# Seven-product second layer for one more token group, and weight sums read from whole chunks

## The chip, the cores and the metric

One NeuronCore of one Trainium2 chip runs the whole kernel. The metric is device time in microseconds (us) of one execution. Matrix work runs on TensorE (PE), elementwise work on VectorE (DVE), ScalarE (ACT) and GpSimd (POOL); SyncE (SP) issues every DMA, in program order, and where an issue has to wait for data or for a free buffer, everything behind it on that queue waits too.

## The reference

```
attn_out = softmax(q kT / 8 + mask) v        # 8 batches x 8 heads, 576 tokens, head size 64
x = attn_out as 4608 tokens x 512            # heads side by side
h = x @ w_in                                 # 512 -> 2048
g = max(h, 0) + alpha * min(h, 0)
out = g @ w_out                              # 2048 -> 512
```

Masks are a window of 32 keys for the first four heads, and every fourth key of the last 128 for the others. All is float32; the kernel gets float32 accuracy from a faster matrix format by splitting each operand into a high and a low part and running three matmuls (high*high, high*low, low*high) for one product.

## The kernel before

Tokens are cut in nine tiles of 512. Tiles 0 to 2 are computed in a first stage, with the conversion of the weights and most of the attention. Tiles 3 to 8 are computed two at a time in `paired_stage`: pairs of tiles at t = 3, 5 and 7, and for each pair two groups (`grp` 0 and 1) of 1024 hidden columns. So there are six rounds, (3,0), (3,1), (5,0), (5,1), (7,0), (7,1), each an h phase (first layer) and a y phase (second layer).

Every h phase multiplies blocks two by two with seven products in place of eight (a Strassen scheme): four units `i`, each with products `q` = 1, 7, 6, 2, 5, 3, 4, and each product six 128x512 matmuls. The products 3 and 4 of a unit run inside the next unit, and those of the last unit inside the y phase, so an h phase holds 26 products of its own. `phase_h` leaves g as it is; `seven_h` also makes the sums of g that a seven-product y phase needs.

The y phase comes in two forms. `phase_y` is the plain one: 4 blocks of output columns x 8 slices x 2 tiles x 3 passes = 192 matmuls, in 32 steps of six (a hook number `n` = 8c + j stands behind each step, and operations that are hung on it are issued there). `seven_y` uses the seven products: 28 steps of six = 168 matmuls, in the order `YSTEPS`. `SEVENS` says which rounds use it: before, the four at t = 5 and 7.

`seven_y` needs sums of blocks of w_out. `second_sum` makes one set of them (set i of 0 to 7; sets 4 to 7 serve `grp` 1, sets 0 to 3 `grp` 0): two loads into a buffer, a run of GpSimd operations, two stores to `wY` in DRAM. The four hook positions of a set are those of first load, second load with the GpSimd work, first store, second store. Both loads and stores are on SP's queue, so a store that waits for GpSimd holds up what is behind it.

The weights of both layers come to PE through a ring of ten 256 KB slots: `take` uses one, `feed` refills the slot just used with the unit ten further on.

The last twelve attention pairs (20 to 31) are spread over the paired stage. A pair has `scores` (PE), `maxima` (DVE, L286 and L289), `exponentials` (ACT, L299), `divisions` and `turns` (DVE, L306 to L314), `values` (PE, L276), `highs` (ACT, L383) and `lows` (DVE, L390), which copy the result out of PSUM. It has one k, one q and one v buffer: a pair loads the next pair's k and q (L201, L202) as soon as its own scores are done, and the next v (L209) after its own values. Before, round (3,0) holds five pairs, a pair every five steps of `phase_y`, values eight steps behind scores; (3,1) three; (5,0) three, one of them in the h phase; (5,1) one, in the h phase. Pairs in an h phase hold two PSUM banks for their values (`NARROW`), the others four.

Of the kernel before, what the change touches and what calls it, by code (L numbers as in the profile page):

```python
# [17 lines left out]
P = 128  # L18
# [7 lines left out]
HB = 9  # L26
# [11 lines left out]
NARROW = (28, 31)  # L38
# [29 lines left out]
def tile_window_attention_prelu_ffn(  # L68
# [34 lines left out]
    marks = dram.tile([2 * NC, 1], F32, name="marks")  # L103
    wY = dram.tile([NFP, 2, P, 2, 2, 2, P], F32, name="wY")
# [301 lines left out]
    class Conversion:  # L406
# [172 lines left out]
    SEVENS = {(NSTD + 2, 0), (NSTD + 2, 1), (NSTD + 4, 0), (NSTD + 4, 1)}  # L579
    for t in range(NSTD, NTILE, 2):  # L580
        for grp in range(NFP // GP):
            seq = []
            for i in range(GP):
                seq.append((i, 1))
                if i:
                    seq += [(i - 1, 3), (i - 1, 4)]
                seq += [(i, 7), (i, 6), (i, 2), (i, 5)]
            units += [wS[grp * GP + i, WBLOCK[q]].rearrange("p a n -> p (a n)") for i, q in seq]
            if (t, grp) in SEVENS:
                for i, q in YSTEPS:  # L590
                    if q == 0:
                        units += [wS[grp * GP + i, WBLOCK[q]].rearrange("p a n -> p (a n)") for q in (3, 4)]
                    elif q in YBLOCK:
                        h, odd = YBLOCK[q]
                        units.append(wY[grp * GP + i, h, :, :, odd].rearrange("p c a n -> p c (a n)"))
# [152 lines left out]
    class Seven(Four):  # L748
# [5 lines left out]
        def __init__(self, t, grp, i):  # L754
            super().__init__(t, grp, i)
            self.turn, self.grp = (grp + i) % 2, grp
# [19 lines left out]
        def s(self, n):  # L776
            k = 3 * self.i + self.ORDER.index(n)
            if k < 8:
                return small(k)
            if "x" not in extra:  # L780
                extra["x"] = const.tile([P, 4, TT], F32, tag="xB0", name=f"extra_{self.id}")
            return extra["x"][:, k - 8]
# [50 lines left out]
    def phase_h(t, grp, hooks):  # L833
# [3 lines left out]
        for i in range(GP):  # L837
            u = Four(t, grp, i)
            u.mm(1)
            u.snap(1)  # L840
            if last:
# [4 lines left out]
            if last:  # L846
                last.low(22)
                last.low(12)
            u.mm(6)
# [3 lines left out]
            for op in hooks.get((i, 6), ()):  # L853
                op()
            u.mm(2)
            u.add(11)
            if last:
                last.low(21)
            u.mm(5)
# [3 lines left out]
            for op in hooks.get((i, 5), ()):  # L863
                op()
# [58 lines left out]
    def phase_y(t, grp, u, hooks):  # L923

        end = grp + 1 == NFP // GP
        for c in range(NC):
# [23 lines left out]
            for tt in range(2):  # L950
                if not end:
# [11 lines left out]
    def seven_y(t, grp, us, hooks):  # L963
# [41 lines left out]

        def H(k, name):
# [5 lines left out]
        def T(k, name):  # L1012
# [17 lines left out]
            (3, 6): [lambda: put(21, "A"), H(3, "T4"), L(3, "T4")],  # L1030
            (3, 5): [lambda: put(22, "A")],
# [4 lines left out]
        for n, (i, q) in enumerate(YSTEPS):  # L1036
# [11 lines left out]
            else:  # L1048
# [3 lines left out]
                for c in range(2):  # L1052
                    for k, (a, e) in enumerate(PASSES):
                        b = 2 * c + a
# [8 lines left out]

    SUMS = {
# [3 lines left out]
    }  # L1068

    def second_sum(i, rooms):  # L1070
# [4 lines left out]
        def load(h):  # L1075
            if not room:
                room.extend(rooms())
            nc.sync.dma_start(
                out=room[h].rearrange("p c o a n -> p c (o a n)"),
                in_=wO[i // GP, 2 * h:2 * h + 2, i % GP].rearrange("c p o a n -> p c (o a n)"))  # L1080

        def last_load():
            load(1)

            def t(q):
                return room[q % 2][:, :, q // 2, 1]

            for x in room:
                nc.gpsimd.tensor_tensor(out=x[:, :, :, 1], in0=x[:, :, :, 0], in1=x[:, :, :, 1], op=ALU.add)  # L1089
            for out, x, y, op in ((3, 1, 3, ALU.add), (1, 0, 1, ALU.subtract), (0, 3, 0, ALU.subtract), (2, 2, 0, ALU.subtract)):  # L1090
                nc.gpsimd.tensor_tensor(out=t(out), in0=t(x), in1=t(y), op=op)  # L1091
            for x in room:
                nc.gpsimd.tensor_copy(out=x[:, :, :, 0].bitcast(F32R), in_=x[:, :, :, 1])
                nc.gpsimd.tensor_tensor(
                    out=x[:, :, :, 1].bitcast(F32R), in0=x[:, :, :, 1], in1=x[:, :, :, 0], op=ALU.subtract)

        def store(h):
            nc.sync.dma_start(
                out=wY[i, h].rearrange("p c o a n -> p (c o a n)"), in_=room[h].rearrange("p c o a n -> p (c o a n)"))
# [3 lines left out]
    def second_sums(hooks, at, spare):  # L1103

        for i, ats, k in SUMS.get(at, ()):
            ops = second_sum(i, (lambda: spare) if k is None else (
                lambda i=i, k=k: [gbuf([P, 2, 2, 2, P], F32, f"wy{i}_{a}", k + a) for a in range(2)]))
            for n, op in zip(ats, ops):
                hooks.setdefault(n, []).append(op)
# [26 lines left out]
    def attention_hooks(hooks, us, start, step):  # L1136
        def put(n, *ops):
            hooks.setdefault(min(n, GF * NC), []).extend(ops)

        lag = max(step + 2, 8)  # L1140
        for k, u in enumerate(us):
            n = start + step * k
            nxt = pairs.index(u) + 1

            def begin(u=u, nxt=nxt):
                u.scores()
                if nxt < len(pairs):
                    pairs[nxt].load_qk()
                u.maxima()
                u.exponentials()  # L1150

            def middle(u=u):
                u.divisions()
                u.turns()

            def end(u=u, nxt=nxt):
                u.values()
                if nxt < len(pairs):
                    pairs[nxt].load_v()
                u.highs()  # L1160
                u.lows()

            put(n, begin)
# [3 lines left out]
    def paired_stage():  # L1167
# [5 lines left out]
        both = const.tile([P, 2, 2, 2, 2, P], F32, tag="xB1", name="wy_spare")  # L1173
        spare = [both[:, h] for h in range(2)]
        early = second_sum(0, lambda: spare)
        late = []
        for t in range(NSTD, NTILE, 2):
            for grp in range(NFP // GP):
                ahead, hooks, seven = {}, {}, (t, grp) in SEVENS

                def put(hooks, u, ats, *tags):
                    for at, op in zip(ats, steps(u, *tags)):
                        hooks.setdefault(at, []).append(op)

                if t == NSTD:
                    us, todo = (todo[:5], todo[5:]) if grp == 0 else (todo[:3], todo[3:])
                    attention_hooks(hooks, us, *{5: (2, 5), 3: (3, 5)}[len(us)])
                    if grp == 0:
                        ahead[0, 5], ahead[1, 6], ahead[2, 5], ahead[3, 6] = ([op] for op in early)
                elif todo:  # L1190
                    free = YPAIRS[1 - grp]
                    put(ahead, todo.pop(0), ((0, 1), (0, 6), (0, 5), (1, 7), (2, 1)), free, free)
                    if grp == 0:
                        two, four = ("a1", "a3"), ("a1", "a3", "y0", "y1")
                        put(hooks, todo.pop(0), (9, 12, 13, 14, 18), two, four)
                        put(hooks, todo.pop(0), (16, 18, 19, 23, 26), ("y0", "y1"), four)
# [16 lines left out]
                second_sums(hooks, (t - NSTD, grp), spare)  # L1213
# [358 lines left out]
```

## Time and profile before

| What | Value |
|---|---|
| Median of three runs | 851.68 us (850.93 to 854.68) |
| The profiled execution: its own time | 848.32 us |
| The profiled execution: its span, first to last instruction | 846.5 us |
| PE busy | 832.0 us, 98% of the span |
| DVE, ACT, POOL busy | 71%, 52%, 16% |
| DMA moved | 182.43 MB, mean 216 GB/s |

The profile is of one execution; the table's first line is of other executions of the same program. Busy shares are means over stages of different kinds, so each stage has to be looked at by itself.

### The profile page before, as it was taken

The page shows a single profiled execution, that of the slowest core. Times are in us where ns is not written, and L with a number is a line of the kernel's source. Part 1 is how long each engine was busy: PE and PEld are TensorE (multiplying, and loading weights), DVE is VectorE, ACT ScalarE, POOL GpSimd, SP SyncE. Part 2 cuts the span into 40 slices and gives each one's busy share as a digit, 9 for nine tenths or more (in the row PEclk, how much of TensorE's full clock was granted, in tenths as well). Part 3 has the DMA queues.
Part 4 walks back from the last instruction along what each step waited for, and adds up shares of the span by engine and source line. Part 5 has one row for each costly group of instructions (what it writes and reads, how often), then busy time and mean ns, then how long its engine had stood idle before and what let it go on. Part 6 is the DMA issues. An engine that isn't in the chain of part 4 may idle for free.

```text
span 846.5 us, 20231 instructions
## 1 busy us (share of the span) xinstructions
PE 832.0 (98%) x8094; PEld 679.3 (80%) x8094; DVE 604.3 (71%) x1024; ACT 437.9 (52%) x1218; POOL 133.6 (16%) x132
## 2 busy tenths in 40 slices
PE   8889999999999999999999999999999999999998
PEld 5677888888888888888788878788888888888886
DVE  5987767676777668686627678698369978843982
ACT  7885766434343543565336642667266436634650
POOL 0000000200405250053900087000300000000000
PEclk9999999999999999999999999999999999999999
DMA  7753444125989965688886787867966686666664
GB/s 258 273 186 100 148 158 145 45 94 173 303 268 336 283 221 171 241 263 251 296 266 193 216 302 263 276 190 239 298 168 191 216 273 192 193 195 194 194 209 142
DMA packets 123515, 182.43 MB, mean 216 GB/s; under 512 B 9758, under 2 KB 69278, under 8 KB 123422
## 3 DMA queue, kind: packets, MB, share of 16 engines
q1 hardware_dynamic: 123422, 181.15, 67.0%
q8 instruction: 64, 1.05, 0.5%
q14 instruction: 29, 0.24, 0.1%
HBM read 139.17 MB, written 41.94 MB: 214 GB/s over the span
## 4 chain that ended last, share of the span: by engine, by line
PE 92%; DMA 3%; POOL 2%; DVE 1%; issue 1%; ACT 1%; SPq 0%; ACTq 0%; DVEq 0%
PE h L456 16%; PE y L504 15%; PE pA L670 15%; PE qA L1055 10%; PE y L935 9%; PE pC L670 8%; PE qC L1055 5%; PE pB L670 4%; PE o L329 3%; PE qB L1055 3%; PE s L227 2%; PE s L251 1%; PE o L276 1%; POOL wy L1091 1%; DMA w_dt.float<-qT 1%
## 5 line engine op out<-in xcount | busy, mean ns | idle before, releaser
L456 PE MATMUL h<-x,w_dt.float32r 128*128 128x512 f32 x576 | 141.3, 394 | 0.9 <-ACT x L383 0.8
L504 PE MATMUL y<-g,w_dt.float32r 128*128 128x512 f32 x576 | 138.3, 389 | 0.0
L456 PEld LDWEIGHTS h<-x,w_dt.float32r 128*128 128x128 f32 x576 | 107.2, 188 | 23.8 <-ACT x L383 0.9
L504 PEld LDWEIGHTS y<-g,w_dt.float32r 128*128 128x128 f32 x576 | 108.0, 188 | 22.4
L299 ACT ACTIVATE pr<-pr,nm 128x64 f32<-128x64 f32 x216 | 72.3, 338 | 57.4 <-DVE nm L289 57.4
L482 ACT CAST g<-m 128x512 fp32r<-128x512 f32 x48 | 29.7, 619 | 74.8 <-DVE m L477 71.8
L670 PE MATMUL pA<-parts_w,ring_w 128*128 128x512 f32 x228 | 56.7, 390 | 0.2 <-ACT stage L904 0.2
L670 PE MATMUL pA<-parts_w,ring_xA 128*128 128x512 f32 x228 | 56.4, 390 | 0.0
L670 PEld LDWEIGHTS pA<-parts_w,ring_w 128*128 128x128 f32 x228 | 42.6, 188 | 9.5 <-ACT stage L904 0.6
L670 PEld LDWEIGHTS pA<-parts_w,ring_xA 128*128 128x128 f32 x228 | 42.7, 188 | 8.9
L811 DVE TENSOR_TENSOR gp<-stage,gp 128x512 fp32r<-128x512 f32 x64 | 42.9, 684 | 2.8 <-ACT gp L807 2.8
L487 DVE TENSOR_TENSOR g<-m,g 128x512 fp32r<-128x512 f32 x48 | 33.6, 700 | 15.5 <-ACT g L482 15.4
L476 DVE TENSOR_SCALAR m<-h,al 128x512 f32<-128x512 f32 x27 | 20.2, 749 | 29.8 <-PE h L456 29.8
L807 ACT CAST gp<-stage 128x512 fp32r<-128x512 f32 x64 | 37.5, 618 | 7.6 <-DVE stage L804 6.4
L299 ACT ACTIVATION_READ_ACCUMULATOR pr<-pr,nm 128x1 f32 x216 | 40.9, 189 | 0.0
L935 PE MATMUL y<-gp,ring_w 128*128 128x512 f32 x168 | 40.7, 394 | 0.0
L1055 PE MATMUL qA<-gp,ring_w 128*128 128x512 f32 x162 | 39.1, 390 | 0.0
L554 POOL TENSOR_TENSOR wsum_xB<-w_dt.float32r 128x512 f32<-128x512 f32 x4 | 5.1, 1295 | 208.8 <-PE h L456 161.9
L935 PE MATMUL y<-gp,ring_xA 128*128 128x512 f32 x156 | 37.3, 393 | 0.0
L1089 POOL TENSOR_TENSOR wy<-wy 128x512 f32<-128x512 f32 x12 | 16.4, 1374 | 128.7 <-DMA wy<-wO 69.4
L935 PEld LDWEIGHTS y<-gp,ring_w 128*128 128x128 f32 x168 | 31.1, 188 | 6.5
L1055 PE MATMUL qA<-gp,ring_xA 128*128 128x512 f32 x150 | 36.2, 390 | 0.0
(177 smaller groups left out, 1687.2 us busy)
## 6 DMA issues: line engine op xcount, KB each, us to landing
ring_xA<-wS SPq DMA_DIRECT2D x67, 256.0 KB, 2.9
ring_w<-wS SPq DMA_DIRECT2D x66, 256.0 KB, 3.6
ring_g<-wS SPq DMA_DIRECT2D x35, 256.0 KB, 3.3
ring_w<-wO SPq DMA_DIRECT2D x34, 256.0 KB, 3.2
ring_xA<-wO SPq DMA_DIRECT2D x33, 256.0 KB, 3.0
wO<-w_dt.float32r SPq DMA_DIRECT2D x32, 256.0 KB, 4.6
wS<-wc SPq DMA_DIRECT2D x16, 512.0 KB, 4.6
k<-kT SPq DMA_DIRECT2D x24, 288.0 KB, 4.6
```

Source lines behind the costliest of these rows:

```text
L299: nc.scalar.activation(out=self.pr[:, r, :], in_=self.ps[r // CUT0][:, r % CUT0, :] if self.onto else self.pr[:, r, :], func=AF.Exp, bias= ...
L329: nc.tensor.matmul(self.po[u][e * D:(e + 1) * D, a:z, :], lhsT=self.v[rows, i, :], rhs=self.pt[rows, a * BK + (BQ if i else 0):z * BK - (B ...
L456: nc.tensor.matmul(ms[t, f], lhsT=weight(0, a, f)[:, c * P:(c + 1) * P], rhs=half(t, c)[:, e, :], start=(c == 0 and n == 0), stop=(c == NC ...
L476: nc.vector.tensor_scalar(out=m, in0=ps, scalar1=0.0, scalar2=al[:, f:f + 1], op0=ALU.min, op1=ALU.mult)
L482: nc.scalar.copy(out=g[:, 0, :], in_=ms[t, f])
L487: nc.vector.tensor_tensor(out=g[:, 1, :], in0=ms.pop((t, f)), in1=g[:, 0, :].bitcast(F32), op=ALU.subtract)
L504: nc.tensor.matmul(ys[t][c], lhsT=weight(1, a, f)[:, c * P:(c + 1) * P], rhs=g[:, e, :], start=(first and n == 0), stop=(last and n == 2),)
L670: nc.tensor.matmul(to, lhsT=w[:, (2 * a + c) * P:(2 * a + c + 1) * P], rhs=part_of(name, e)[:, c * TT:(c + 1) * TT], start=start and c == ...
L807: nc.scalar.copy(out=self.pair(n)[:, 0], in_=self.whole(n))
L811: nc.vector.tensor_tensor(out=p[:, 1], in0=self.whole(n), in1=p[:, 0].bitcast(F32), op=ALU.subtract)
L935: nc.tensor.matmul(ys2[tt], lhsT=w[:, k * P:(k + 1) * P], rhs=g[:, e], start=j == 0 and n == 0, stop=j == GF - 1 and n == 2)
L1055: nc.tensor.matmul(named(to)[c], lhsT=w[:, b * P:(b + 1) * P], rhs=rhs[:, e], start=begins and k == 0, stop=i == GP - 1 and k == 2, skip_g ...
```

## The change

1. Round (3,1) joins `SEVENS`: its h phase becomes `seven_h` and its y phase `seven_y`.
2. The seven-product sets are made for it in time: sets 4 and 5 in the h phase of (3,0), sets 6, 7, 0 and 1 in its y phase, sets 2 and 3 in the h phase of (5,0). Before, sets 0 to 3 were made in (3,0), 4 to 6 in (3,1), 7 in (5,0).
3. A set is no longer made from the stored high and low parts, which GpSimd had to add again (L1089). Each w_out chunk is stored whole, as `wW`, when it is converted; the loads of a set are half as big. `wY` is laid out so that a unit is one piece for each partition; `b` in `seven_y` follows.
4. (3,0) takes seven attention pairs in its y phase, one every four steps, values six steps behind scores; pair 27 goes to the h phase of (3,1) and becomes narrow; (5,0) and (5,1) keep theirs.
5. Temporaries: the third set of temporaries that does not fit (`further`) goes to other buffers; in (3,0), two blocks of partial sums go to DRAM (`part`) and are read back late in the y phase of (3,1) (`again`).

```diff
-NARROW = (28, 31)
+NARROW = (27, 28, 31)
...
+    wW = dram.tile([NFP, P, 2, 2, 2, P], F32, name="wW")
...
         def low(self):
             nc.vector.tensor_tensor(
                 out=self.dst[1], in0=self.a.bitcast(F32), in1=self.dst[0].bitcast(F32), op=ALU.subtract)
+            if self.which:
+                nc.sync.dma_start(
+                    out=wW[self.f // 2, :, :, self.f % 2].rearrange("p h c n -> p h (c n)"),
+                    in_=self.a.bitcast(F32).rearrange("p (h n) -> p h n", h=2))
...
-    SEVENS = {(NSTD + 2, 0), (NSTD + 2, 1), (NSTD + 4, 0), (NSTD + 4, 1)}
+    SEVENS = {(NSTD, 1), (NSTD + 2, 0), (NSTD + 2, 1), (NSTD + 4, 0), (NSTD + 4, 1)}
...
+        def further(self, k):
+
+            if self.t == NSTD and k in (1, 2):
+                if k == 2:
+                    return pr0.rearrange("q j k -> q (j k)")[:, :TT]
+                if "pt" not in extra:
+                    extra["pt"] = att.tile([P, HB * BK], F32, tag="pt", name=f"extra_{self.id}")
+                return extra["pt"][:, :TT]
+            if self.t == NSTD or self.grp == 0:
+                return partial(*((0, 1), (2, 0), (3, 0), (1, 1))[k])
...
+                if not end and tt and c < 2 and (t, 1) in SEVENS:
+                    o = ffp.tile([P, TT], F32, tag="m", name=f"ob_{t}_{c}_{tt}", bufs=5)
+                    nc.vector.tensor_copy(out=o, in_=ys2[tt])
+                    nc.sync.dma_start(out=part[c], in_=o)
+                    continue
...
             nc.sync.dma_start(
-                out=room[h].rearrange("p c o a n -> p c (o a n)"),
-                in_=wO[i // GP, 2 * h:2 * h + 2, i % GP].rearrange("c p o a n -> p c (o a n)"))
+                out=room[h][:, :, 1].rearrange("p o c n -> p o (c n)"), in_=wW[i, :, h].rearrange("p o c n -> p o (c n)"))
...
-            for x in room:
-                nc.gpsimd.tensor_tensor(out=x[:, :, :, 1], in0=x[:, :, :, 0], in1=x[:, :, :, 1], op=ALU.add)
...
-                if t == NSTD:
-                    us, todo = (todo[:5], todo[5:]) if grp == 0 else (todo[:3], todo[3:])
-                    attention_hooks(hooks, us, *{5: (2, 5), 3: (3, 5)}[len(us)])
-                    if grp == 0:
-                        ahead[0, 5], ahead[1, 6], ahead[2, 5], ahead[3, 6] = ([op] for op in early)
+                if (t, grp) == (NSTD, 0):
+                    us, todo = todo[:7], todo[7:]
+                    attention_hooks(hooks, us, 1, 4, 6)
+                    put(ahead, ((0, 6), (0, 5), (2, 1), (2, 7)), second_sum(4, at_place("xB1")))
+                    four = second_sum(5, at_place("xB1"))
+                    put(ahead, ((3, 1), (3, 6)), four[:2])
+                    put(hooks, (3, 4), four[2:])
+                    put(hooks, (6, 8, 11, 12), second_sum(6, at_buffers(6, 1)))
+                    put(hooks, (8, 10, 15, 16), second_sum(7, at_buffers(7, 3)))
+                    put(hooks, (12, 14, 19, 20), second_sum(0, at_place("xB1")))
+                    put(hooks, (16, 18, 23, 24), second_sum(1, at_buffers(1, 1)))
...
+                    put(ahead, ((1, 1), (1, 6), (2, 7), (2, 2)), second_sum(2, at_place("xB0")))
+                    four = second_sum(3, at_place("xB0"))
+                    put(ahead, ((3, 7), (3, 2)), four[:2])
+                    put(hooks, (2, 3), four[2:])
```

## Rows read from the trace of the kernel before

**Rows 1.** Page, part 1: busy time, share of the span and instructions of each engine.

```profile
PE 832.0 (98%) x8094; PEld 679.3 (80%) x8094; DVE 604.3 (71%) x1024; ACT 437.9 (52%) x1218; POOL 133.6 (16%) x132
```

**Rows 2.** Page, part 4: the chain that ended last, by engine.

```profile
PE 92%; DMA 3%; POOL 2%; DVE 1%; issue 1%; ACT 1%; SPq 0%; ACTq 0%; DVEq 0%
```

**Rows 3.** Chain in order of time: start, us, twelve matmuls in a row.

```profile
77.92 2.72 PE h L456 x12
```

**Rows 4.** Windows by phase: (3,0) whole, (3,1) h, y, (5,0) h, y, (5,1) h.

```profile
core 0: us, PE busy (x) PEld busy (x) DVE busy (x) ACT busy (x) POOL busy (x), PEclk, DMA share, GB/s
343.98:437.62 93.64, 93.64 (x1142) 75.92 (x1141) 59.79 (x108) 45.12 (x158) 41.13 (x40) 1.00 0.85 282
437.62:472.98 35.36, 35.36 (x158) 29.28 (x157) 23.24 (x35) 19.59 (x36) 0.00 (x0) 1.00 0.68 195
472.98:526.44 53.46, 53.46 (x674) 43.30 (x673) 40.28 (x64) 23.44 (x83) 34.40 (x29) 1.00 0.79 271
526.44:565.52 39.08, 38.74 (x313) 31.48 (x312) 31.06 (x51) 23.13 (x56) 1.59 (x2) 1.00 0.77 239
565.52:611.14 45.62, 45.62 (x494) 37.12 (x493) 30.17 (x57) 23.88 (x74) 9.51 (x10) 1.00 0.83 260
611.14:649.62 38.48, 38.41 (x313) 31.56 (x312) 28.46 (x50) 24.08 (x60) 0.00 (x0) 1.00 0.64 182
```

**Rows 5.** Timeline, (5,0) h: ACT and PE behind a store of sums.

```profile
533.00 0.59 ACT L904 COPY stage<-pA 128x512 f32<-128x512 f32 x1 [4.44 <-DMA wY<-wy]
...
533.64 3.02 PE L670 MATMUL pA<-parts_w,ring_w 128*128 128x512 f32 x12 [0.23 <-ACT stage L904]
```

**Rows 6.** Timeline, (3,0) y: a pair's values, copies out of PSUM, scores.

```profile
408.57 1.12 PE L276 MATMUL o<-pt,v 32*64 32x32 f32 x84
409.63 3.02 PE L935 MATMUL y<-gp,ring_xA 128*128 128x512 f32 x12
...
409.74 0.19 DVE L390 COPY raw_xA<-o 128x32 f32<-128x32 f32 x1 [3.56 <-PE o L276]
409.85 0.48 DVE L390 COPY raw_xB<-o 128x128 f32<-128x128 f32 x2
...
410.24 0.68 DVE L953 COPY py<-y 128x512 f32<-128x512 f32 x1
...
412.57 0.97 PE L251 MATMUL s<-k,q 64*32 64x64 f32 x72
```

**Rows 7.** Timeline of POOL: first and last operation after L1089, three sets.

```profile
365.05 4.18 POOL L1091 TENSOR_TENSOR wy_spare<-wy_spare 128x256 f32<-128x256 f32 x4
...
373.24 1.63 POOL L1094 TENSOR_TENSOR wy_spare<-wy_spare 128x512 fp32r<-128x512 f32 x1
...
407.56 0.73 POOL L1091 TENSOR_TENSOR wy<-wy 128x256 f32<-128x256 f32 x1
...
413.92 1.30 POOL L1094 TENSOR_TENSOR wy<-wy 128x512 fp32r<-128x512 f32 x1
...
516.53 1.69 POOL L1091 TENSOR_TENSOR wy<-wy 128x256 f32<-128x256 f32 x1
...
526.83 1.28 POOL L1094 TENSOR_TENSOR wy<-wy 128x512 fp32r<-128x512 f32 x1
```

**Rows 8.** Page, part 6: DMA issues, KB each, median us to landing.

```profile
ring_w<-wS SPq DMA_DIRECT2D x66, 256.0 KB, 3.6
...
wO<-w_dt.float32r SPq DMA_DIRECT2D x32, 256.0 KB, 4.6
```

**Rows 9.** Tile q, from 380 to 640 us.

```profile
DMA to landing us min/median/max: 4.2/4.7/5.7
```

**Rows 10.** Timeline of SP in (3,0) y: issues of k and q.

```profile
422.78 0.33 SPq L201 DMA_DIRECT2D k<-kT  x1
423.17 1.72 SPq L202 DMA_DIRECT2D q<-qT  x1
```

**Rows 11.** Timeline of DVE in (3,0) y: one operation, POOL idle, then busy.

```profile
393.53 0.76 DVE L308 TENSOR_TENSOR pr<-pr,rs 128x576 f32<-128x576 f32 x1
...
401.49 1.67 DVE L308 TENSOR_TENSOR pr<-pr,rs 128x576 f32<-128x576 f32 x1
```

**Rows 12.** Timeline of DVE: operations of the token parts, POOL idle and busy.

```profile
520.91 1.76 DVE L655 TENSOR_TENSOR parts_w<-raw_xA,parts_w 128x1024 fp32r<-128x1024 f32 x1
...
696.32 1.22 DVE L655 TENSOR_TENSOR parts_w<-raw_xB,parts_w 128x1024 fp32r<-128x1024 f32 x1 [1.48 <-ACT parts_w L652]
```

**Rows 13.** Windows of the first stage, where the weights are converted.

```profile
90.00:130.00 40.00, 40.00 (x178) 33.15 (x177) 29.45 (x47) 25.30 (x44) 0.00 (x0) 1.00 0.52 180
```

More of the change, by code (lines that the diff above doesn't have):

```diff
@@ L838, in phase_h, with more @@
             u = Four(t, grp, i)
+            def more(q):
+                for op in hooks.get((i, q), ()):
+                    op()
             u.mm(1)
             u.snap(1)
+            more(1)
             if last:
@@ L848, in phase_h @@
                 last.low(12)
+            more(7)
             u.mm(6)
@@ L852, in phase_h @@
                 last.high(21)
-            for op in hooks.get((i, 6), ()):
-                op()
+            more(6)
             u.mm(2)
@@ L858, in phase_h @@
                 last.low(21)
+            more(2)
             u.mm(5)
@@ L862, in phase_h @@
             u.add(22)
-            for op in hooks.get((i, 5), ()):
-                op()
+            more(5)
             last = u
@@ L1004, in whole_first, with again @@
                     nc.sync.dma_start(out=outT[c * P:(c + 1) * P, t * TT:(t + 1) * TT], in_=out(11, c))
+        def again():
+            if t == NSTD:
+                for c in range(2):
+                    nc.sync.dma_start(out=out(12, c), in_=part[c])
         def H(k, name):
@@ L1092, in last_load, with at_buffers, at_place, rooms @@
             for x in room:
-                nc.gpsimd.tensor_copy(out=x[:, :, :, 0].bitcast(F32R), in_=x[:, :, :, 1])
-                nc.gpsimd.tensor_tensor(
-                    out=x[:, :, :, 1].bitcast(F32R), in0=x[:, :, :, 1], in1=x[:, :, :, 0], op=ALU.subtract)
+                nc.gpsimd.tensor_copy(out=x[:, :, 0].bitcast(F32R), in_=x[:, :, 1])
+                nc.gpsimd.tensor_tensor(out=x[:, :, 1].bitcast(F32R), in0=x[:, :, 1], in1=x[:, :, 0], op=ALU.subtract)
         def store(h):
             nc.sync.dma_start(
-                out=wY[i, h].rearrange("p c o a n -> p (c o a n)"), in_=room[h].rearrange("p c o a n -> p (c o a n)"))
+                out=wY[i, h].rearrange("p o a c n -> p (o a c n)"), in_=room[h].rearrange("p o a c n -> p (o a c n)"))
         return lambda: load(0), last_load, lambda: store(0), lambda: store(1)
[L1103 to L1109, printed above, removed]
+    def at_buffers(i, k):
+        return lambda: [gbuf([P, 2, 2, 2, P], F32, f"wy{i}_{a}", k + a) for a in range(2)]
+    def at_place(tag):
+        def rooms():
+            if tag not in sets:
+                sets[tag] = const.tile([P, 2, 2, 2, 2, P], F32, tag=tag, name=f"wy_{tag}")
+            return [sets[tag][:, h] for h in range(2)]
+        return rooms
+    sets = {}
     def steps(u, *tags):
@@ L1134, in steps, with attention_hooks @@
         return begin, lambda: u.exponentials(0, CUT0), lambda: u.exponentials(CUT0), middle, end
-    def attention_hooks(hooks, us, start, step):
+    def attention_hooks(hooks, us, start, step, lag):
         def put(n, *ops):
-            hooks.setdefault(min(n, GF * NC), []).extend(ops)
-        lag = max(step + 2, 8)
+            hooks.setdefault(n, []).extend(ops)
         for k, u in enumerate(us):
+            begin, first, second, middle, end = steps(u, *((("a0", "a2"), ABANKS) if k == 0 else (ABANKS[2:], ABANKS) if k % 2 else (ABANKS[:2], ABANKS)))
             n = start + step * k
[L1143 to L1163, printed above, removed]
+            put(n, begin, first, second)
             put(n + step - 1, middle)
@@ L1190, in paired_stage @@
                 elif todo:
                     free = YPAIRS[1 - grp]
[L1192 to L1196, printed above, removed]
+                    put(ahead, ((0, 1), (0, 6), (0, 5), (1, 7), (2, 1)), steps(todo.pop(0), free, free))
```

26 lines of the change are left out of this document (13 added, 13 removed), and 3 rows, old and new, of the table SUMS.

## Prediction

> **What bounds the kernel now.** I read the page's busy shares first, then the chain that ended last, then windows cut at the phases, then the timelines of PE, POOL, DVE and SP in the rounds that change. PE is busy for 98% of the span [rows 1] and makes up 92% of the chain [rows 2]: the kernel ends when PE has worked off its queue. The engines beside it matter only where one makes PE wait. So the change is counted in PE time, and then each place where PE could be made to wait is looked at.
>
> PE's unit of work is a step of six 128x512 matmuls. Twelve in a row take 2.72 us [rows 3], so a step is 1.36 us and a matmul 0.227. The windows [rows 4] can be rebuilt from that. The h phase of (3,1) has 26 steps and no attention: 26 x 1.36 = 35.36, to the hundredth what its window shows. Round (3,0) has 26 + 2 + 32 = 60 steps, 81.60, and five pairs: (93.64 - 81.60) / 5 = 2.41 us of PE time for a pair. The y phase of (3,1) gives the same price: 53.46 - 34 x 1.36 = 7.22 for three pairs, 2.41 each. A pair inside an h phase costs more: (5,1) h is 38.48 - 35.36 = 3.12. And (5,0) h, the same work, takes 39.08, 0.60 more: there ACT sat 4.44 us until a store of sums had landed, and PE lost time behind it [rows 5]. In this accounting PE has no other slack in these rounds.
>
> **The change, part by part.**
>
> *The seven-product y of (3,1).* 192 matmuls become 168: 24 x 0.227 = **-5.44 us**. The h phase keeps its 26 steps.
>
> *Pair 27* moves from a y phase (2.41) to an h phase (3.12): **+0.71**. The two other pairs moved from (3,1) to (3,0) keep their price of 2.41, as both are y phases.
>
> *The sets leave the y phase of (3,1).* The store that ACT waited for at the start of (5,0) [rows 5] is then long done: **-0.60**, the difference of the two h phases above.
>
> *The seventh pair of (3,0)* has its values at hook 31, behind the last step. The next thing on PE is the first product of (3,1), which writes a bank that DVE copies these values out of. Before, one more step stood between. There [rows 6] PE goes on at 409.63 after a pair's values, and DVE's copies end at 409.85 + 0.48 = 410.33, 0.70 later; after its first copy alone (409.93) it would be 0.30. I take **+0.70**, as this pair's share in that bank is several pieces. These four give -4.63.
>
> *Seven pairs, one every four steps, in (3,0).* A pair comes every 4 x 1.36 + 2.41 = 7.85 us in place of 9.21. DVE and ACT have room: 59.79 and 45.12 us busy of 93.64 there [rows 4]. What gets tight is SP's queue. k and q of the next pair are issued once this pair's scores are done, and needed 7.85 - 1.1 = 6.7 us later (2.41 split as 0.97 to 1.12 [rows 6] gives 1.1 for scores, 1.3 for values). q takes 4.7 us to land, 5.7 at most [rows 9], and its own issue can take 1.72 [rows 10]. So little is left if anything stands in front of it, and the new stores do: hooks 12, 16 and 20 hold a set's second store, which waits for the end of that set on POOL, and the loads of k and q at hooks 13, 17 and 21 are behind them.
>
> Times from the start of the y phase: pair k (from 0) is scored at 5.44 + 7.85k - 1.3 for k of 1 or more, so pairs 4, 5 and 6 at 35.5, 43.4 and 51.2. Set 6's second load (hook 8) is queued behind the spill of the first block, which needs pair 0's values (end near 17.1), DVE's copies (0.7) and the block's copy (0.68) [rows 6]; issued near 18.9, landed near 22.3 (256 KB take 3.6 in the ring [rows 8], a little less at best). POOL then makes sets 6, 7, 0 and 1 back to back. Without L1089, which the change removes, a set takes p = 415.22 - 407.56 = 7.66 us in (3,0) y, 9.82 in (3,0) h and 11.58 late in (3,1) y, from start to end of its operations [rows 7]. Between POOL's end and q's issue come a store, a load or none, a feed and k, some 1.3 to 1.7 us at 0.33 to 0.4 each [rows 10], and q lands 4.7 later. So q of pair 4 is there at 28.7 + p, of pair 5 at 28.7 + 2p, of pair 6 at 28.3 + 3p, and PE's total loss is the largest of p - 6.8, 2p - 14.7 and 3p - 22.9. With p = 7.66 that is 0.9, and with landings of 5.7 it is 1.9; with p = 9.82 it is 6.6. From below it is nothing, if q is quicker by the 0.5 that its fastest landing (4.2) shows, and the load of set 6 too. POOL runs here beside the same DVE work as in the 7.66 row, only denser, so I take p near that row and a landing between the two: **+1.5**.
>
> DVE and POOL disturb each other: the multiplication L308 takes 0.76 alone and 1.67 beside POOL [rows 11]. The Trainium skill, "SBUF — State Buffer", section "Who interferes with whom", says why: a DVE operation with two SBUF inputs and a GpSimd operation that reads SBUF share one read interface, and the one that comes second waits for the whole of the other. By that rule each pair's L308 would add up to 0.76 to a set: p = 8.4, a loss of 2.3 in place of 0.9. The rows agree that DVE waits; they show 7.66 with such a pair beside it.
>
> *(5,0) h* now has pair 28, five operations of the token parts that came earlier before, and POOL's sets 2 and 3. DVE was busy 31.06 of 39.08 [rows 4]. Three of the five are DVE's, 1.22 each alone and 1.76 beside POOL [rows 12]: 3.7 to 5.3 us more, so 35 to 36 of 38.5. That fits in sum, but in unit 0 products 3 and 4 have to wait for ACT's copies, which stand behind exponentials and one such operation more. Between 0 (all covered) and 1.5 (one ACT and one DVE operation of the token parts late) I take **+0.4**. Set 3's last store must land before a unit of it is fed; by p = 11.58 that is just in time, so nothing.
>
> *The 16 stores of whole chunks* cost SP about 0.4 us each where the DMA share is 0.52 [rows 13], and land in 4.6 [rows 8]; the buffer they hold is reused over a step (5.44) later. I take 0; the other bound is 1 us, for the first three, which fall in the start. If DMA were full there, each would cost its own transfer. The new layout of `wY` and L1089's removal have no PE time of their own: POOL idles 84% of the span [rows 1].
>
> Sum: -5.44 + 0.71 - 0.60 + 0.70 + 1.5 + 0.4 = **-2.7 us**. The profiled execution took 848.32 (span 846.5), so 845.6. The median of the runs is 851.68; taken off that, **849.0 us**.
>
> **The rivals.**
>
> *All is hidden* (A): q always lands in time and (5,0) h runs free; -4.63 remains, to -5.3 if the values at hook 31 are covered too: 846.4 to 847.1. For it: PE waits for almost nothing today. Against: the 0.9 that the best row of p gives.
>
> *POOL's chain holds SP* (B), slower: place, the second store of sets 6, 7 and 0 in (3,0) y. If a set takes 9.82 as in the h phase, the loss is 6.6 and the time 851.68 - 4.63 + 6.6 + 0.4 = 854.1; at 11.58 it is 11.8, and 859.3. It makes the kernel slower than before from p = 9.1, and by over 0.5% from p = 10.5. Against: three sets in this very phase took about 7.66.
>
> *DVE binds (5,0) h* (C): if DVE's operations there all took their long form, about 1.5 to 4 us would be lost: 850 to 852.5.
>
> **How the numbers follow.** 0.5% is 4.3 us, about what a measurement of this kernel can tell from no change. My forecast 0.48 (losses of 0.5 to 4 in all, 847.5 to 851), A 0.32, C 0.10, B 0.10. A is faster by over 0.5%; the forecast and C are within it; B is slower, nearly all of it by over 0.5%. So faster 0.32, same 0.58, slower 0.10. The range goes from A's lower end, 846.4, to 853.0, which holds C and leaves out B.
>
> **What would show it.** (3,1) y without attention should be 28 + 2 steps, 40.8 us, and (3,1) h 38.5 plus the loss at its first product. (3,0) should be 81.60 + 7 x 2.41 = 98.5, and what is above it is loss: in PE's waits at the scores, with DMA as the releaser, and in SP's waits for POOL at the stores. POOL's sets should take 7 to 8.5 us there. (5,0) h should be 38.5 plus at most 1.5. I would be wrong most of all if SP does not get held (then A), or if p is above 9 (then B).

## The result, and the profile after

The changed kernel takes **862.88 us** (median of 4 runs, 861.6 to 863.85) against 852.03 for the kernel before in the same job: 1.0143 of it, 95% interval 1.0117 to 1.0169. It is slower by 10.9 us. The forecast was 849.0 with a range up to 853.0. The profiled execution took 863.11 (span 861.3), against 848.32.

The page's busy shares, against [rows 1]:

```profile
PE 834.3 (97%) x8070; PEld 677.9 (79%) x8070; DVE 624.5 (73%) x1052; ACT 444.2 (52%) x1232; POOL 108.2 (13%) x116
```

The page's chain by engine, against [rows 2]:

```profile
PE 84%; DVE 8%; ACT 3%; DMA 3%; issue 2%; SPq 0%; ACTq 0%; DVEq 0%
```

PE has 24 matmuls fewer, and is busy longer, which points to a lower clock in places. DVE had 1% of the chain and has 8% now. Windows of the kernel after, cut at the phases as in [rows 4]: (3,0) y, (3,1) h, (3,1) y, (5,0) h, (5,0) y; (3,0) h, from 349.08, takes 35.36 as planned:

```profile
384.44:458.77 74.33, 67.01 (x1297) 52.44 (x1296) 43.43 (x95) 31.86 (x166) 35.72 (x40) 0.95 0.80 265
458.77:497.35 38.58, 38.52 (x312) 31.64 (x313) 29.24 (x53) 23.91 (x61) 0.00 (x0) 1.00 0.69 202
497.35:538.15 40.80, 40.80 (x181) 33.78 (x180) 34.42 (x49) 18.00 (x28) 0.00 (x0) 1.00 0.76 242
538.15:578.37 40.22, 39.20 (x313) 31.19 (x312) 35.75 (x54) 24.66 (x58) 8.17 (x8) 1.00 0.79 255
578.37:625.91 47.54, 46.27 (x493) 37.17 (x492) 34.14 (x57) 23.51 (x74) 8.91 (x8) 1.00 0.74 236
```

Against before: (3,0) took 109.69 in place of 93.64, where its two more pairs account for 4.8, so 11.2 are loss; (3,1) took 79.38 in place of 88.82, which is the gain, 9.44; (5,0) took 87.76 in place of 84.70. That is +9.7 us. The other 5.1 of the profiled difference lie before (3,0), which starts at 349.08 in place of 343.98 [rows 4]; but before's profiled execution lies 3.7 below the median of its runs, so in the medians little over 1 us of it is left (10.9 - 9.7), if the rounds take the same in other executions, which no trace here shows. From (5,1) on the phases are as before.

**The opening of (3,0) y.** Timeline of PE after: start, time taken, operation and, in brackets, the idle time before it with what ended it:

```profile
398.17 0.96 PE L252 MATMUL s<-k,q 64*32 64x64 f32 x72 [1.52 <-issue]
399.06 2.99 PE L958 MATMUL y<-gp,ring_w 128*128 128x512 f32 x12
402.98 0.30 PE L277 MATMUL o<-pt,v 32*64 32x32 f32 x4 [0.93 <-DVE pt L315]
...
404.43 1.20 PE L277 MATMUL o<-pt,v 32*64 32x32 f32 x78 [0.56 <-DVE pr L287]
405.56 4.34 PE L958 MATMUL y<-gp,ring_w 128*128 128x512 f32 x12
```

Timeline of POOL after, same stretch:

```profile
387.64 3.19 POOL L1116 TENSOR_TENSOR wy_xB<-wy_xB 128x256 f32<-128x256 f32 x4 [13.90 <-DMA wy_xB<-wW]
...
394.65 1.61 POOL L1119 TENSOR_TENSOR wy_xB<-wy_xB 128x512 fp32r<-128x512 f32 x1
```

Timeline of DVE after:

```profile
392.32 4.50 DVE L743 TENSOR_TENSOR gp<-n,gp 128x512 fp32r<-128x512 f32 x3
396.74 0.48 DVE L287 SCALAR_TENSOR_TENSOR pr<-s,mask_sb 128x320 f32<-128x320 f32 x1
...
397.65 0.41 DVE L287 SCALAR_TENSOR_TENSOR pr<-s,mask_sb 128x256 f32<-128x256 f32 x1
```

The same three multiplications by DVE before, with POOL idle:

```profile
387.10 1.89 DVE L738 TENSOR_TENSOR gp<-n,gp 128x512 fp32r<-128x512 f32 x3
```

POOL makes set 5 from 387.64 to 396.26, just where DVE opens the phase. DVE's three multiplications take 4.50 in place of 1.89; the maxima of the first pair, behind them on DVE, start at 396.74, some six us after its scores were done. The second pair's scores write a bank that these maxima read: DVE leaves it at 397.65 + 0.41 = 398.06, and PE, stopped for 1.52, goes on at 398.17. (The profile says "issue", the times say DVE; in the kernel with sets 0 and 1 later, below, the profile puts the same stop, 1.09 there, down to DVE's pr L287.) Three stops at the values follow, of 0.93, 0.29 and 0.56; with the 1.52 that is 3.30 us. And then twelve matmuls that elsewhere take 3 us take 4.34. The first pair's scores also stand a step earlier than before (hook 1 in place of 2), and the pairs closer together; an experiment has to tell this from POOL.

**The clock.** Windows after, from 405.0 and from 428.9 (us, PE, PEld, DVE, ACT, POOL, granted clock, DMA share, GB/s):

```profile
405.00:408.40 3.40, 3.40 (x51) 2.76 (x41) 2.25 (x7) 3.04 (x17) 0.00 (x0) 0.50 0.46 145
...
428.90:432.30 3.40, 3.40 (x63) 2.69 (x44) 1.73 (x4) 1.46 (x9) 2.92 (x4) 0.50 1.03 398
```

After the stops the granted clock is 0.50 (1.2 GHz) for 3.4 us, and then 1.00 (2.4 GHz) again. Twelve matmuls in it took 1.3 us longer; half of the 3.4, an estimate for all of PE's work in it, is 1.7. That was lost each of the two times.

**The fifth pair's q.** Timeline of PE, then of SP, after:

```profile
428.49 1.19 PE L252 MATMUL s<-k,q 64*32 64x64 f32 x72 [2.84 <-DMA q<-qT]
...
443.06 0.45 PE L277 MATMUL o<-pt,v 32*64 32x64 f32 x28 [0.55 <-issue]
```

```profile
417.24 2.77 SPq L1122 DMA_DIRECT2D wY<-wy  x2
...
421.94 0.42 SPq L203 DMA_DIRECT2D q<-qT  x1
```

q is issued at 421.94, behind SP's hold at the stores of set 6, and lands 6.4 us later by the chain, where I had counted 4.7 to 5.7 (the view that gave [rows 9] has 4.3 to 6.1 for the landings of this round that it shows). DMA is full there; the view adds up the packets' times, so a share can pass 1. Windows after, from 420 on:

```profile
420.00:426.00 6.00, 5.66 (x104) 4.20 (x102) 3.69 (x11) 3.98 (x25) 5.54 (x8) 1.00 0.89 273
426.00:432.00 6.00, 3.51 (x78) 2.88 (x79) 2.52 (x6) 1.16 (x7) 3.75 (x5) 0.74 1.01 348
432.00:438.00 6.00, 6.00 (x133) 4.60 (x135) 2.90 (x9) 2.70 (x18) 4.04 (x5) 0.98 1.01 344
438.00:444.00 6.00, 5.45 (x170) 4.29 (x149) 2.17 (x7) 3.48 (x21) 5.45 (x8) 1.00 0.98 374
```

Before, slices of this length lay between 0.69 and 0.97 in (3,0) y, and no stop fell in them; the fullest, and the one behind it:

```profile
415.00:421.00 6.00, 6.00 (x106) 4.85 (x105) 3.04 (x11) 3.85 (x24) 5.65 (x7) 1.00 0.97 334
421.00:427.00 6.00, 6.00 (x96) 4.50 (x95) 3.69 (x7) 3.10 (x19) 4.14 (x4) 1.00 0.70 215
```

So (3,0) lost 3.30 at the opening, 2.84 at q, 0.55 at a stop called "issue", 0.63 at the first product of (3,1), and 2.6 to 3.4 to the clock: 9.9 to 10.7 of the 11.2.

**(5,0).** Timeline of POOL after, where its y phase begins, and then of DVE:

```profile
581.93 4.29 POOL L1116 TENSOR_TENSOR wy_xB<-wy_xB 128x256 f32<-128x256 f32 x4 [16.27 <-DMA wy_xB<-wW]
```

```profile
582.10 1.23 DVE L828 TENSOR_TENSOR gp<-stage,gp 128x512 fp32r<-128x512 f32 x1
...
590.08 1.77 DVE L828 TENSOR_TENSOR gp<-stage,gp 128x512 fp32r<-128x512 f32 x1
591.77 0.68 DVE L828 TENSOR_TENSOR gp<-py,gp 128x512 fp32r<-128x512 f32 x1
```

The same operation takes 1.2 to 1.8 while POOL makes set 3, and 0.68 as soon as it is done; POOL's four operations take 4.29, where those of set 5 took 3.19.

### The profile page after: what moved, and what is told of

It is laid out like the page before. It is cut to its first block, busy times and chain, and to the rows that moved or that the text cites. A ratio compares the mean times of both kernels' runs of the same rounds, so it can differ in the third digit from the quotient of the medians.

```text
span 861.3 us, 20294 instructions
## 1 busy us (share of the span) xinstructions
PE 834.3 (97%) x8070; PEld 677.9 (79%) x8070; DVE 624.5 (73%) x1052; ACT 444.2 (52%) x1232; POOL 108.2 (13%) x116
## 4 chain that ended last, share of the span: by engine, by line
PE 84%; DVE 8%; ACT 3%; DMA 3%; issue 2%; SPq 0%; ACTq 0%; DVEq 0%
PE y L509 15%; PE h L461 15%; PE pA L675 13%; PE qA L1089 11%; PE pC L675 6%; PE qC L1089 5%; PE y L958 4%; PE pB L675 3%; PE o L330 3%; PE qB L1089 3%; PE s L228 2%; DVE gp L828 2%; PE o L277 1%; ACT pr L300 1%; PE s L252 1%
## 5 line engine op out<-in xcount | busy, mean ns | idle before, releaser
L828 DVE TENSOR_TENSOR gp<-stage,gp 128x512 fp32r<-128x512 f32 x80 | 56.2, 717 | 3.4 <-ACT gp L824 3.4
L824 ACT CAST gp<-stage 128x512 fp32r<-128x512 f32 x80 | 46.8, 618 | 9.8 <-DVE stage L821 8.3
L1089 PE MATMUL qA<-gp,ring_xA 128*128 128x512 f32 x192 | 46.4, 390 | 0.0
L1089 PE MATMUL qA<-gp,ring_w 128*128 128x512 f32 x192 | 46.1, 389 | 0.0
L1089 PEld LDWEIGHTS qA<-gp,ring_w 128*128 128x128 f32 x192 | 36.0, 188 | 7.5
L1089 PEld LDWEIGHTS qA<-gp,ring_xA 128*128 128x128 f32 x192 | 35.9, 188 | 7.5
L1116 POOL TENSOR_TENSOR wy_xB<-wy_xB 128x256 f32<-128x256 f32 x20 | 17.5, 875 | 189.1 <-DVE pr L309 111.8
L287 DVE SCALAR_TENSOR_TENSOR pr<-s,mask_sb 128x320 f32<-128x320 f32 (+1 forms) x48 | 21.7, 452 | 17.3 <-PE s L252 12.9
L1012 DVE TENSOR_TENSOR py<-qA,py 128x512 f32<-128x512 f32 x22 | 15.1, 691 | 24.7 <-PE qA L1089 24.7
```

The lines of the kernel that those rows point to most:

```text
L287: nc.vector.scalar_tensor_tensor(out=self.pr[:, a:z], in0=self.ps[i], scalar=SCALE, in1=mask_sb[:, self.mask + a:self.mask + z], op0=ALU.m ...
L824: nc.scalar.copy(out=self.pair(n)[:, 0], in_=self.whole(n))
L828: nc.vector.tensor_tensor(out=p[:, 1], in0=self.whole(n), in1=p[:, 0].bitcast(F32), op=ALU.subtract)
L1089: nc.tensor.matmul(named(to)[c], lhsT=w[:, b * P:(b + 1) * P], rhs=rhs[:, e], start=begins and k == 0, stop=i == GP - 1 and k == 2, skip_g ...
```

## The experiments

Each kernel is the changed one with the edit shown, but one (the stores alone), which starts from the kernel before. "Ratio" is to the kernel before, with its 95% interval.

### Are the stores of whole chunks what delays the start?

```diff
-            if self.which:
+            if self.which and self.f >= 6:
...
+        if f < 6:
+            nc.sync.dma_start(
+                out=wW[f // 2, :, :, f % 2].rearrange("p h c n -> p h (c n)"),
+                in_=weight(1, 0, f).bitcast(F32).rearrange("p (h n) -> p h n", h=2))
```

> The changed kernel, with the whole-chunk stores of the first six w_out chunks taken out of the start and put where the other weights are saved, some 200 us later; for those six chunks the stored words are the high part alone, so the sums of three sets leave the low part out. Theory (the stores wait on SP's queue for DVE's conversion, and hold the loads of q, k, v and weights behind them): the first product of round (3,0) starts near 344 us again in place of 349.1, and the time falls by 4 to 6 us, to 857 to 859. Rival (the start varies by itself, with PE's instruction fetch): it starts at 348 to 350 and the time stays within 2 us of 862.9.

The words stored for these six chunks are the high part alone. 859.39 us, ratio 1.0091 (1.0059 to 1.0123); (3,0) starts at 345.9.

The same six stores, issued from ACT's queue:

```diff
-                nc.sync.dma_start(
+                (nc.scalar if self.f < 6 else nc.sync).dma_start(
```

> The changed kernel, with the same six early stores issued from ScalarE's queue in place of SP's; bytes, place and data unchanged. Theory (SP is held): as without them, round (3,0) starts near 344 and the time falls by 4 to 6 us. Rival (the bytes themselves delay the loads of the start, whoever issues them): the start stays at 348 to 350, the time within 2 us of 862.9.

860.27, ratio 1.0106 (1.0078 to 1.0134); start at 347.4. These are 3.5 and 2.6 us below the changed kernel, but neither settles it: the variants further down, which leave these stores as they are, start anywhere from 345.7 to 349.4. The third says more: the kernel before with the 16 stores and nothing else.

```diff
+    wW = dram.tile([NFP, P, 2, 2, 2, P], F32, name="wW")
...
+            if self.which:
+                nc.sync.dma_start(
+                    out=wW[self.f // 2, :, :, self.f % 2].rearrange("p h c n -> p h (c n)"),
+                    in_=self.a.bitcast(F32).rearrange("p (h n) -> p h n", h=2))
```

> The kernel before, with the 16 stores of whole w_out chunks added and nothing else; nobody reads them. Theory (at the start they hold SP's queue and fill the DMA engines): slower than before by 2 to 4 us, round (3,0) starting at 346 to 349. Rival (the start varies by itself, between 344 and 349): same as before within 1 us.

852.17, ratio 1.0003 (0.9985 to 1.0022); start at 344.49. By themselves the stores cost nothing, and the theory that they make the start late falls; a cost that comes only together with the rest of the change is not excluded.

### POOL beside DVE, at the two openings

Set 5 is only cast; its sums and subtractions are left out:

```diff
+            if i in (5,):
+                for x in room:
+                    nc.gpsimd.tensor_copy(out=x[:, :, 0].bitcast(F32R), in_=x[:, :, 1])
+                return
```

> The changed kernel, with the GpSimd work of set 5 cut to its two casts (the four sums and two subtractions are left out), so that GpSimd is idle while DVE finishes the last unit at the start of the y phase of (3,0). Theory (DVE and GpSimd block each other there; pair 0's maxima start 5 us late and pair 1's scores wait for a bank they read): the waits of 1.5, 0.9, 0.3 and 0.6 us at the first two pairs go, with the fall of the clock behind them; the y phase goes from 73.7 to 68 to 70 us. Rival (a pair every four steps is too quick for the chain of maxima, exponentials and transpose by itself): the waits stay, y phase 72 us or more.

861.17, ratio 1.0107 (1.0057 to 1.0158). The opening is free, though the pairs stand as in the changed kernel: of its stops one of 0.56 is left, and DVE's three multiplications are back at 1.89. Timeline of DVE, then the window of (3,0) y:

```profile
390.24 1.89 DVE L743 TENSOR_TENSOR gp<-n,gp 128x512 fp32r<-128x512 f32 x3
```

```profile
382.48:454.26 71.78, 65.59 (x1298) 51.37 (x1296) 40.59 (x95) 31.87 (x166) 28.21 (x33) 0.98 0.81 273
```

But the phase only went from 74.33 to 71.78: the waits for q grew from 2.84 to 3.65 + 1.19. What was won ahead is given back at the next limit.

The same for sets 2 and 3 (`if i in (2, 3):`), which are made in (5,0):

> The changed kernel, with the GpSimd work of sets 2 and 3 cut to its casts (sums and subtractions left out), so that round (5,0) has hardly any GpSimd work. Theory (DVE and GpSimd block each other in (5,0) h and at the start of its y phase): the h phase goes from 40.2 to 38.5 to 39.2 us and the y phase from 47.5 to 45.6 to 46.2. Rival (the token parts that now lie in the same h phase as a pair are too much for ACT and DVE without GpSimd): h stays at 39.8 or more and the copies at the start of y stay late.

859.5, ratio 1.008 (1.0059 to 1.01). Windows of (5,0) h and y:

```profile
537.50:576.63 39.13, 38.50 (x314) 31.41 (x312) 33.92 (x54) 24.87 (x58) 1.71 (x2) 1.00 0.84 262
576.63:622.24 45.61, 45.61 (x493) 37.12 (x492) 30.58 (x57) 23.86 (x74) 1.41 (x2) 1.00 0.79 247
```

87.76 has become 84.74: 3.0 us of (5,0) were POOL's additions beside DVE. The Trainium skill, "SBUF — State Buffer", section "Who interferes with whom", has the cause: a DVE operation with two SBUF inputs contends with a GpSimd operation that reads SBUF, as its second input comes through the read interface that the two engines share. Both experiments agree: the three multiplications went from 4.50 to 1.89, and in (5,0) y the multiplications that take 1.22 to 1.77 beside set 3 take 0.69 when its additions are left out, and once 1.10, beside one of the casts.

### Is it SP's hold, or the full DMA?

Stores moved behind the loads of the next pair:

```diff
-                    put(hooks, (6, 8, 11, 12), second_sum(6, at_buffers(6, 1)))
-                    put(hooks, (8, 10, 15, 16), second_sum(7, at_buffers(7, 3)))
+                    put(hooks, (6, 8, 13, 14), second_sum(6, at_buffers(6, 1)))
+                    put(hooks, (8, 10, 17, 18), second_sum(7, at_buffers(7, 3)))
...
-                    put(hooks, (16, 18, 23, 24), second_sum(1, at_buffers(1, 1)))
+                    put(hooks, (18, 20, 27, 28), second_sum(1, at_buffers(1, 1)))
```

> The changed kernel, with the stores of sets 6, 7 and 1 moved two to four hooks later, so that the loads of k and q at hooks 13 and 17 stand ahead of them on SP's queue. Theory (the store that waits for GpSimd holds q back): the wait of 2.8 us for q at pair 4 goes, with the fall of the clock behind it; the y phase of (3,0) goes from 73.7 to 69 to 70.5. Rival (the DMA engines are full, at a share of 0.98 there, and q is late whatever is ahead of it): a wait of 1.5 us or more for q stays.

860.61, ratio 1.0106 (1.0069 to 1.0143). Timeline of SP: q is issued ahead of the stores.

```profile
415.87 0.42 SPq L203 DMA_DIRECT2D q<-qT  x1
416.35 0.91 SPq L1122 DMA_DIRECT2D wY<-wy  x2
```

No wait for q is left, and (3,0) y takes 73.53 all the same, against 74.33. Timeline of PE:

```profile
423.47 0.31 PE L252 MATMUL s<-k,q 64*32 64x64 f32 x5 [0.90 <-issue]
...
432.78 0.81 PE L252 MATMUL s<-k,q 64*32 64x64 f32 x59 [1.80 <-issue]
...
438.84 0.45 PE L277 MATMUL o<-pt,v 32*64 32x64 f32 x28 [1.54 <-issue]
```

These three stops, 4.24 us, lie inside blocks of scores and values whose first matmuls have gone through, so their data is there. Window of that kernel, and the DMA view from 436 to 438 us (queue, packets, MB, share of 16 engines):

```profile
430.00:436.00 6.00, 4.20 (x87) 3.16 (x86) 2.68 (x6) 1.26 (x8) 1.31 (x1) 1.00 1.02 374
```

```profile
q1 hardware_dynamic: 426, 0.78, 103.5%
q8 instruction: 1, 0.02, 3.1%
```

The DMA engines are full with data, and among it goes one packet of a queue called "instruction"; one such packet starts 0.7 to 1.5 us ahead of each of these stops. So SP's hold alone is not what sets the length of the phase. What the records point to is that PE waits for its own instructions, which come over the same full engines. For this speaks that the stops keep their places in the program: the one five matmuls before the end of the fifth pair's scores comes in three kernels here (0.90 above, 0.58 and 0.77 in the next two), and the one in that pair's values in three as well, the changed kernel among them. Against it speaks that such packets come every few us in the kernel before too, where the DMA view from 419 to 420.6 us, in the slice of 0.97 shown above, has

```profile
q8 instruction: 1, 0.02, 3.6%
```

and no stop follows; and that at the start of the changed kernel PE stops inside such blocks for 3.00 and 2.17 us at DMA shares of 0.74 and 0.47. So that the packet is PE's next code, and that full engines make it late, is read from coincidence and not shown.

### Less DMA and less POOL in (3,0): sets 0 and 1 a round later

```diff
-                    put(hooks, (12, 14, 19, 20), second_sum(0, at_place("xB1")))
-                    put(hooks, (16, 18, 23, 24), second_sum(1, at_buffers(1, 1)))
+                if (t, grp) == (NSTD, 1):
+                    put(hooks, (11, 13, 20, 21), second_sum(0, at_buffers(0, 1)))
+                    put(hooks, (13, 15, 24, 25), second_sum(1, at_buffers(1, 3)))
```

> The changed kernel, with sets 0 and 1 made in the y phase of (3,1) in place of that of (3,0): 3 MB fewer for the DMA engines in (3,0). Theory now (the DMA engines are full for 18 us of this phase, and both q and PE's own instructions come late): the wait for q of 2 to 3.6 us, the stops inside attention blocks and the clock falls behind them go, and the y phase of (3,0) goes from 73.5 to 69 to 70.5 us (the waits at the first two pairs stay); the y phase of (3,1) stays at 40.8, or grows by up to 2 if DVE and GpSimd block each other there. Rival (SP held by a store that waits for GpSimd): set 6's stores are as before, so the wait for q at pair 4 stays at 2 us or more, y phase 72.5 or more.

861.91, ratio 1.0097 (1.0061 to 1.0133). Windows of (3,0) y and (5,0) h:

```profile
383.59:453.54 69.95, 65.70 (x1297) 51.51 (x1296) 42.01 (x95) 31.48 (x166) 22.90 (x24) 0.98 0.75 236
532.92:577.80 44.88, 39.76 (x314) 31.06 (x312) 39.27 (x55) 24.68 (x59) 17.18 (x14) 1.00 0.87 297
```

(3,0) y gains 4.38. The fifth pair does not wait for q, and the sixth for 0.18, though SP is held at the stores of set 6 as long as in the changed kernel (2.77):

```profile
415.64 2.76 SPq L1122 DMA_DIRECT2D wY<-wy  x2
```

So the hold alone did not make the wait of 2.84; fuller DMA engines, and one load more ahead of q, had a part in it. (3,1) y keeps its 40.79 though two sets are made in it. But (5,0) h loses 4.66: SP is held for 11.4 us by POOL at the stores, and two units of weights come late behind it, 1.6 and 1.4. The groups of waits (waiter, releaser: total, count, longest), one of PE's, then SP's:

```profile
PE pA L675 <- DMA ring_w<-wS: 1.6, 1, 1.6
```

```profile
SPq L1122 <- POOL wy L1119: 11.4, 4, 3.9
```

That is the mechanism that I had forecast for (3,0), here in another place; the kernel after the next tests it.

Next, with set 5 moved away from the opening as well:

```diff
-                    put(ahead, ((3, 1), (3, 6)), four[:2])
-                    put(hooks, (3, 4), four[2:])
-                    put(hooks, (6, 8, 11, 12), second_sum(6, at_buffers(6, 1)))
-                    put(hooks, (8, 10, 15, 16), second_sum(7, at_buffers(7, 3)))
+                    put(hooks, (2, 4, 11, 12), four)
+                    put(hooks, (6, 8, 15, 16), second_sum(6, at_buffers(6, 1)))
+                    put(hooks, (10, 14, 19, 20), second_sum(7, at_buffers(7, 3)))
```

> As the kernel with sets 0 and 1 made later, and set 5 taken from the end of the h phase to hooks 2 and 4 of the y phase, sets 6 and 7 behind it. Theory (two causes, one beside the other: GpSimd beside DVE at the opening, and full DMA engines): both go, y phase of (3,0) near 63.8 to 65.5 us, and the whole kernel at 851 to 854. Rival (the spacing of four steps is too quick in any case): y phase above 68, kernel above 856.

858.46, ratio 1.008 (1.0055 to 1.0105): slower than expected by 4 us and more, since (3,0) y still lost some and (5,0) h, 44.81, kept SP's hold. Windows of (3,0) y, then three slices of it:

```profile
382.04:449.67 67.63, 64.48 (x1297) 50.42 (x1296) 40.00 (x95) 31.79 (x166) 21.40 (x24) 1.00 0.79 248
```

```profile
406.00:412.00 6.00, 6.00 (x174) 4.62 (x172) 4.00 (x10) 3.43 (x20) 5.54 (x8) 1.00 0.93 274
412.00:418.00 6.00, 5.49 (x106) 4.32 (x102) 3.39 (x11) 4.16 (x25) 0.96 (x1) 1.00 1.00 365
418.00:424.00 6.00, 5.24 (x91) 4.02 (x90) 3.84 (x9) 1.25 (x8) 4.82 (x6) 1.00 1.01 355
```

With 6.7 less than in the changed kernel, the phase now never sees the lower clock. The stops at "issue" that are left, 0.51 and 0.77, lie in the two slices where DMA is full, and none in the one at 0.93; a third, of 0.61, lies in a slice at 0.95.

Then the stores of sets 0 and 1 behind the feeds that they had held up:

```diff
-                    put(hooks, (11, 13, 20, 21), second_sum(0, at_buffers(0, 1)))
-                    put(hooks, (13, 15, 24, 25), second_sum(1, at_buffers(1, 3)))
+                    put(hooks, (11, 13, 25, 26), second_sum(0, at_buffers(0, 1)))
+                    behind_h = second_sum(1, at_buffers(1, 3))
+                    put(hooks, (13, 15), behind_h[:2])
+                if (t, grp) == (NSTD + 2, 0):
+                    put(ahead, ((0, 2), (0, 5)), behind_h[2:])
```

> As the kernel with set 5 and sets 0 and 1 later, with the four stores of sets 0 and 1 moved behind: set 0's to hooks 25 and 26, set 1's into the h phase of (5,0). Theory (in that kernel the stores waited for GpSimd 11.8 us in all on SP's queue, and the ring's feeds behind them came late: PE waited 1.0 and 1.3 us for weights in (5,0) h): these two waits go, (5,0) h falls from 44.8 to 40 to 42 us, the kernel to 853.5 to 856. Rival (the DMA engines are full there, or ACT and DVE bind): h stays above 43.5. Beating the kernel before would take the loss in (5,0) as well, so I do not expect it.

855.98, ratio 1.0058 (1.0043 to 1.0072), the lowest here, though this interval and that of the kernel above overlap. Windows of (5,0) h and y:

```profile
530.09:570.88 40.79, 39.02 (x313) 31.18 (x312) 37.33 (x54) 24.77 (x58) 17.06 (x15) 1.00 0.87 301
570.88:618.55 47.67, 46.23 (x493) 37.21 (x492) 34.13 (x57) 23.41 (x74) 9.45 (x8) 1.00 0.73 236
```

(5,0) h is 4.0 shorter by the place of two sets' stores; what (5,0) still takes more, 88.46 against 84.70 before, is near what POOL beside DVE cost above, and was not taken apart further.

Last, POOL's operations cut in half, on top of that, so that DVE would wait for less at a time:

```diff
-                nc.gpsimd.tensor_tensor(out=t(out), in0=t(x), in1=t(y), op=op)
+                for c in range(2):
+                    nc.gpsimd.tensor_tensor(out=t(out)[:, c], in0=t(x)[:, c], in1=t(y)[:, c], op=op)
```

(the cast and the subtraction behind it likewise)

> The same, with each GpSimd operation of a set cut into two halves, 16 in place of 8. If DVE, when it meets GpSimd, waits for the whole of the GpSimd operation in flight, shorter ones make its waits shorter: (5,0), h and y together, falls by 0.5 to 2 us against the kernel with whole operations. If they share by turns in any case, or the added overhead of each operation weighs as much, it stays within 0.4 us or grows.

857.82 (851.12 to 862.17), ratio 1.0066 (1.0045 to 1.0088): no better. In its profile, which is of the slowest of its executions, (5,0) y takes 53.79, with waits of 1.86 for weights and 2.79 for q that the others lack; it tells nothing on the size of operations.

## Why the prediction was wrong

**What held.** (3,1) y took the 40.80 forecast, and (3,1) h 38.58 where 38.5 was: the 24 matmuls' 5.44, pair 27's 0.71 and the 0.60 of the store of sums came as worked out. PE's stop at the first product of (3,1) was 0.63 for 0.70. The stores cost nothing by themselves, as taken. And the number on which rival B hung was right: sets 6 and 7 took 7.66 and 7.5 us, below the 9.1 from which B decides. Neither sign of being wrong came: SP was held, and p was not above 9. Most of what went wrong in (3,0) stood in no rival.

**The step that failed: "Seven pairs, one every four steps, in (3,0)", +1.5.** It measured 10.6 (11.2 less the 0.63 above). I saw one way to lose time there, SP held at the stores while POOL makes a set, and priced PE's wait by p alone. That wait came: 2.84 for 0.9 to 1.9, as q landed in 6.4 and not in 4.7 to 5.7. But with the hold taken away the phase was hardly shorter (73.53 for 74.33), and with less to move the wait went although the hold stayed: seven pairs, five sets and the feeds fill the DMA engines, and that I had not counted. Of the three landings behind [rows 9], the 4.2 and the 4.7 lie in (3,1) and (5,0), at mean shares of 0.79 and 0.77 [rows 4]; the only one in (3,0) y is the 5.7. I priced a denser round with a landing between. What makes PE stop at "issue" once the hold is gone stays open.

Two terms were missing from that step. Set 5 was costed at nothing, since POOL idles 84% of the span; I counted what POOL and DVE do to each other as time of POOL's alone, in p, and not what DVE loses when it is the limit, though [rows 11] showed the price. The opening is where DVE is the limit, and 3.3 us went there; without set 5's additions all but 0.56 came back. And no stop was counted with what follows it: twice the clock fell to half for 3.4 us, 1.3 to 1.7 us each.

**The same mistake, smaller: (5,0), +0.4.** It measured 3.7 (87.76 against 38.48 + 45.62). I had rival C with 1.5 to 4 for DVE's token parts in long form, and gave it 0.10; its size was right and its place half: 1.7 were lost in the h phase and 1.9 in the y phase, 1.4 of them up to its first scores. 3.0 of the 3.7 went away with POOL's additions (84.74); the 0.6 that stayed is near the term.

**The sum.** In the profile: 9.1 too little for (3,0), 3.3 for (5,0), and 5.1 in the start that I did not have make up 17.5, the distance from 845.6 to 863.11. The start stays open: (3,0) began at 345.7 to 349.4 in ten profiled executions of the changed kernel and its variants, and at 343.98 and 344.49 in two of the kernel before and of that with the stores alone. So it is not the stores alone. The difference opens at one block of values; PE before, and then after:

```profile
28.36 1.35 PE L329 MATMUL o<-pt,w_dt.float 32*64 32x32 f32 x76 [1.19 <-issue]
```

```profile
32.29 0.55 PE L330 MATMUL o<-pt,w_dt.float 32*64 32x64 f32 x24 [3.00 <-issue]
```

The 18 matmuls behind it start 3.13 later than before, and take 5.96 in place of 4.37, at a granted clock of 0.51 from 32.9 to 36.3 us, where before has 1.00. By 72 us all of the 5.10 is there: twelve matmuls start at 71.84 that started at 66.74. The change has no step there but these stores; what else delays that block was not found.

**Where the gain went.** The 9.44 of (3,1) are real. They were paid for with work pressed into (3,0) and (5,0): undoing that step by step gave ratios of 1.0143, 1.0080 and 1.0058 (the intervals of the last two overlap), and no version here got back to the kernel before.

## What to carry to other kernels

When work is moved off the bottleneck's path into an earlier round, look at that round's DMA share and at the neighbours of each operation, not only at the idle share of the engine that gets it: here POOL, which idles 84% of the span, took time from DVE where DVE was the limit, and landings read at shares of 0.77 and 0.79 (4.2 and 4.7 us) did not hold near 1.0 (6.4). Of a stop of the bottleneck, count also the lower clock that can follow it. And where one hold is removed, ask what the next limit is: three times here the freed time was taken by another wait.

## What was not expected of the hardware

- In (3,0) y, PE stopped for 0.5 to 1.8 us inside blocks whose data was there, where the DMA share was 0.95 to 1.03 in the slice around (2 to 6 us), with a packet of an instruction queue shortly ahead; the cause is not shown. The Trainium skill, "DMA: Bandwidth & Descriptors", section "Issuing engines are not separate DMA queues", says that DMAs run on the same 16 engines whichever engine issued them. The DMA view adds that packets of an instruction queue take time on them as well (3.1% in the 2 us above).
- Stops of 2.84, and of 1.78 in three pieces within 3 us (1.52 four us ahead), were each followed by 3.4 us at a granted clock of 0.50; stops of 0.5 to 0.8 (the kernel with set 5 and sets 0, 1 moved) were not, nor were those of 0.90, 1.80 and 1.54, which lie 7.5 and 4.5 us apart, in the kernel with the stores behind.
- Three 128x512 multiplications by DVE with both inputs in SBUF take 1.89 alone and 4.50 beside POOL. POOL's time varies as well: the four additions and subtractions of a set took 3.19 there, and 4.29 at the start of (5,0) y.
